# An attention and mixer kernel: a head pair's turned q, k and decay rows reach their operand tiles by plain transfers instead of VectorE copies

## The chip, the cores and the metric

The kernel runs on one core of a Trainium2 chip. The metric is device time in microseconds (us). An execution that is profiled gives, besides its time, a trace of every instruction on the core's engines: TensorE (PE, with its weight loads as PEld), VectorE (DVE), ScalarE (ACT), GpSimd (POOL) and SyncE (SP), and of the transfers that SP and POOL issue. SP computes nothing here; it issues transfers, one after the other, and holds at one that must wait.

## The reference, cut to what matters

Eight batches, eight heads, 576 tokens, 64 elements a head; then a mixer over tokens of low rank (32) and a feed-forward part of width 2048 on the 512 channels.

```python
scores = scale * q @ k.T                       # per batch and head, 576 x 576
cum    = cumsum(max(s, 0))
bias   = -(cum[:, None] - cum[None, :])
scores = where(causal, -1e9, scores + min(bias, 0))
attn   = exp(scores - max) / sum
x      = attn @ v                              # 8 x 576 x 512
u      = x + (x.T @ U @ V).T                   # mixing over tokens
out    = u + max(u @ w_ch1, 0) @ w_ch2
```

## The kernel before, in words

**Pairs.** The 64 heads of all batches are worked in 32 pairs; pair n belongs to batch n // 4. For each pair there is an operand tile, a *slot*: 64 rows of q and of k with the elements on the partitions (turned), and under them four *decay rows*, with which the product of TensorE gives q times k and the cumulated bias at once. From pair 8 on three slots are used in turn, so pair n takes the slot of pair n - 3 and must wait for that pair's scores.

**How a slot is filled.** The decay rows come from a scratch tensor in HBM by two small transfers on SP (`rows_of`, L302). For batches 0 to 3, TensorE turns q and k, and DVE or ACT copies them from PSUM (`transposes`). From pair 16 on (`ZB * PB`, batches 4 to 7) POOL's transfers load q and k of both heads side by side (`load_pairs`, L121), one transposing transfer on SP turns a whole pair (`turn_pair`, L358) into one of three *landings*, tiles of 128 partitions with one head in the lower and one in the upper half, and `part_pair` (L366) copies each half into the slot's lower 64 partitions by a DVE copy.

**The main loop** goes over n from 8 to 33. In iteration n it issues the transposing transfer of pair n + 3, the slot of pair n + 1, the scores of pair n (`scores`, L429; exp on ACT, the causal mask on DVE, L373), and the values of pair n - 1 (`values`, L493, scaled by DVE into `x_sb`, L503). For batches from 2 on, `values` also issues a transposing transfer on SP that turns the pair's x (`xT<-x_sb`, L510), four to a batch. In the second pair of a batch (n = 13, 17, 21, 25, 29), `seqmix` of the batch before runs: PE computes the low-rank product, and DVE adds it to the turned x (L547, `uT<-...,xT`). It needs all four turned x of that batch, the last of which belongs to the pair whose values were computed just before. Between these steps PE is filled with the feed-forward part of an earlier batch (`chanmix`: L662 the first product, L720 the second, by quarters; DVE sums at L698 and L734; sends of the results `out_dram<-o_sb` on SP, L744; the turned u, `u_sd<-uT`, on SP, L1026).

**Who sets the order.** PE and POOL run in the order in which the program is written (`in_program_order` at the end). DVE, ACT and SP are written in program order for batch 0 only; after that the framework's scheduler orders their instructions by data, priority and its own estimates, and the semaphores are placed for that order. On each engine instructions then go strictly in that order: what stands behind a waiting instruction waits too. A transfer on SP also waits for the one eight transfers before it to have landed, since SP has eight completion semaphores in turn.

**Buffers named below.** The results leave through three `o_sb` tiles in turn; a batch group has four quarters, so the fourth quarter's first DVE write waits until the first quarter's send has landed.

Of the kernel before, what the change touches and what calls it, by code (L numbers as in the profile page):

```python
# [16 lines left out]
ALU = mybir.AluOpType  # L17


def in_program_order(tc, first, engines):  # L20

    traced, last = tc.nc.cur_bb.bb.instructions, {}
    for ins in list(traced)[first:]:
        if ins.engine not in engines:
            continue
        prev = last.get(ins.engine)
        if prev is not None:
            tc.add_manual_dep(
                ins,
                prev.name,  # L30
                mybir.DependencyInfo(
                    mybir.DependencyClass.NoSync, mybir.DependencyReason.DATA
                ),
                reason="in_program_order",
            )
        last[ins.engine] = ins


# [1 line left out]
def kernel(  # L40
# [12 lines left out]
    nc = tc.nc  # L53
# [10 lines left out]
    NP = BH // 2  # L64
# [288 lines left out]
    def landing(n):  # L353
        return landings[(n - ZB * PB) % 3]

    def turn_pair(n):
        b, hp = divmod(n, PB)
        nc.sync.dma_start_transpose(  # L358
            out=landing(n).rearrange("p (a m) -> p a m", m=TR),
            in_=by_pairs(b)[:, hp].rearrange("p c t two d -> p (c t two d)"),  # L360
        )

    def part_pair(n):
        rows_of(n)
        for hh in range(2):
            nc.vector.tensor_copy(slot_of(n)[0:D, hh, 0 : 2 * S], landing(n)[ds(hh * D, D)])  # L366
            yield

    def mask(dst, n_tiles, w, on_pool=False):
        if on_pool:  # L370
# [110 lines left out]
    def values(n, pT):  # L481
        b, hp = divmod(n, PB)
        if hp == 0:
            x_of[b] = work.tile([128, PB, 5, 128], BF16, tag="x_sb", name="x_sb")
            if b >= FT:
                xT_of[b] = work.tile([128, 4, 640], BF16, tag="xT", name="xT", bufs=1)
        x_sb, vt = x_of[b], v_slot(b)
        for hh in range(2):
            h = 2 * hp + hh
            po = pwork()[:, : 5 * (D + 1)].rearrange("p (i d) -> p i d", i=5)  # L490
            for i in range(5):
                for j in range(i + 1):
                    nc.tensor.matmul(  # L493
                        po[:, i, :],
                        lhsT=pT[:, hh, ds(place(j, i), 128)],
                        rhs=vt[:, j, h, :],
                        start=(j == 0),
                        stop=(j == i),
                        skip_group_check=True,
                    )  # L500
            rec = work.tile([128, 5, 1], FP32, tag="rec", name="rec", bufs=4)
            nc.vector.reciprocal(rec, po[:, :, D : D + 1])  # L502
            nc.vector.tensor_tensor(  # L503
                x_sb[:, hp, :, ds(hh * D, D)],
                po[:, :, 0:D],
                rec.to_broadcast([128, 5, D]),
                op=ALU.mult,
            )
            if hh == 1 and b >= FT:
                nc.sync.dma_start_transpose(  # L510
                    out=xT_of[b][:, hp, :].rearrange("p (t m) -> p t m", t=5),
                    in_=x_sb[:, hp, :, :].rearrange("p t d -> p (t d)"),
                )
            yield


# [725 lines left out]
    for n in range(2 * PB, NP + 2):  # L1242
# [11 lines left out]
                step(mixing)  # L1254
                fill_with(2)
        if n > 2 * PB and n + 1 < NP:
            for at, _ in enumerate((transposes if n + 1 < ZB * PB else part_pair)(n + 1)):
                step_fill()
                if at == 0:
                    step(mixing)  # L1260
        if 2 * PB + 1 < n < NP:
            for at, _ in enumerate(scores(n, pT_of(n))):
                step_fill()
                if at == 1:
                    step(mixing)
        for _ in mixing:
            fill_with(1)
        if hp == 1 and FT < b < B:
# [76 lines left out]
```

## Time and profile before

| | us |
|---|---|
| median of the runs (lowest, highest) | 357.67 (357.37 to 358.89) |
| the profiled execution's own time | 359.33 |
| its span, first to last instruction | 357.6 |
| PE busy in it | 343.6 |
| DVE busy | 264.4 |
| ACT busy | 207.6 |
| POOL busy | 112.6 |

"Busy" leaves out instructions that only issue transfers or wait; what SP does is therefore read from its own queue's rows. A row of groups such as `L366 DVE COPY slot<-turned 64x1152 ... x12 | 5.7, 478 | 1.0 <-PE pwork L429 0.8` reads: line 366, on DVE, writing `slot` from `turned`, twelve of them, 5.7 us busy in all, 478 ns each, and 1.0 us of idle time of DVE just before them, of which 0.8 ended with PE's line 429. A row of waits such as `A <- B: 3.1, 2, 2.8` reads: A waited for B 3.1 us in all, in two places, 2.8 us at the longest. A row of the chain or of the queue begins with the start and the length in us. The names `qk_sd` in rows of L358 and L366 are two of the three landings, which lie in spare columns of the tiles that hold q and k; `turned` is the third.

### The profile page before, as it was taken

What the parts mean: (1) busy time and instruction counts of PE and PEld (TensorE: products, weight loads), DVE (VectorE), ACT (ScalarE), POOL (GpSimd) and SP (SyncE); (2) the same over time, 40 slices, a digit from 0 to 9 for tenths busy, and PEclk for the clock granted to TensorE, in tenths of its full rate; (3) what the DMA queues carried; (4) which work ended last, traced back from release to release, by engine and by line L of the source; (5) the groups of instructions that cost most, each with busy time, mean ns of one, the idle gap of its engine ahead of it and who ended that gap; (6) DMA issues with size and microseconds to landing.
All of it is one profiled execution on the core that took longest, in us unless ns stands there. A gap on an engine that the chain in (4) does not pass through costs nothing.

```text
span 357.6 us, 9219 instructions
## 1 busy us (share of the span) xinstructions
PE 343.6 (96%) x3770; PEld 247.9 (69%) x3770; DVE 264.4 (74%) x584; ACT 207.6 (58%) x314; POOL 112.6 (31%) x158
## 2 busy tenths in 40 slices
PE   7999999999998999999999997899899999999996
PEld 3685656665587657775678565776588558888885
DVE  8686776779789849883798465983788779676774
ACT  4786965847762577348833874347752554675710
POOL 8897274447356603850366040000000000000000
PEclk9999999999999999999999999999999999999999
DMA  6999999999999999999599999472033525010022
GB/s 100 163 193 203 177 187 121 146 144 97 192 101 171 162 168 88 167 176 159 72 120 160 204 118 90 73 163 57 0 57 83 115 30 120 29 60 31 29 90 88
DMA packets 163713, 42.06 MB, mean 118 GB/s; under 512 B 148312, under 2 KB 162040, under 8 KB 163672
## 3 DMA queue, kind: packets, MB, share of 16 engines
q0 software_dynamic: 101744, 18.45, 80.7%
q1 hardware_dynamic: 61640, 22.83, 36.0%
q8 instruction: 29, 0.48, 0.6%
q10 hardware_dynamic: 288, 0.20, 0.2%
q14 instruction: 12, 0.10, 0.1%
HBM read 37.25 MB, written 9.70 MB: 131 GB/s over the span
## 4 chain that ended last, share of the span: by engine, by line
PE 77%; DVE 12%; ACT 5%; DMA 4%; issue 2%; POOL 0%; DVEq 0%; ACTq 0%; POOLq 0%
PE pwork L662 22%; PE pwork L720 12%; PE quarter L720 9%; PE pscore L429 9%; PE pwork L493 7%; PE parts L950 6%; PE pwork L681 3%; DVE uT L547 3%; DMA xT<-x_sb 2%; ACT pT L447 2%; PE pwork L322 2%; DVE slot L345 2%; DVE o_sb L734 2%; DVE slot L698 2%; ACT hT L1039 1%
## 5 line engine op out<-in xcount | busy, mean ns | idle before, releaser
L662 PE MATMUL pwork<-uT,w_sb 128*128 128x512 bf16 x432 | 106.6, 379 | 1.1 <-ACT hT L1039 0.9
L447 ACT ACTIVATE pT<-pscore 128x1024 bf16<-128x1024 f32 x56 | 56.5, 1031 | 52.7 <-PE pscore L429 52.3
L1039 ACT ACTIVATE hT<-pwork 128x512 bf16<-128x512 f32 x108 | 65.4, 610 | 37.1 <-PE pwork L662 36.3
L662 PEld LDWEIGHTS <-w_sb 128*128 128x128 bf16 x448 | 38.7, 98 | 38.0 <-issue 1.3
L429 PE MATMUL pscore<-slot 68*128 68x320 bf16 (+1 forms) x500 | 55.4, 246 | 0.6 <-ACT hT L447 0.3
L185 POOL DMA_DIRECT2D v_slot<-in_v_dram x40 | 33.8, 860 | 67.9 <-PE pwork L493 57.6
L429 PEld LDWEIGHTS <-slot 68*128 68x128 bf16 x564 | 41.8, 97 | 18.2 <-issue 1.2
L373 DVE TENSOR_TENSOR pT<-pT,keep 128x512 bf16<-128x512 bf16 (+1 forms) x81 | 28.5, 353 | 31.7 <-ACT pT L447 28.7
L720 PEld LDWEIGHTS <-hT 128*128 128x128 bf16 x496 | 46.7, 98 | 7.5 <-issue 0.8
L493 PEld LDWEIGHTS <-pT 128*128 128x128 bf16 x870 | 32.5, 97 | 10.2 <-issue 4.4
L493 PE MATMUL pwork<-v_slot,pT 128*128 128x65 bf16 x870 | 35.8, 193 | 3.8 <-DVE uT L547 3.1
L503 DVE TENSOR_TENSOR x_sb<-pwork,rec 128x320 bf16<-128x320 f32 x64 | 31.2, 489 | 1.5
L459 ACT ACTIVATE pT<-pscore 128x1024 bf16<-128x1024 f32 x29 | 30.4, 1047 | 2.6 <-PE pscore L429 2.4
L720 PE MATMUL pwork<-w_sb,hT 128*128 128x256 bf16 x240 | 30.1, 273 | 0.3 <-DVE o_sb L734 0.3
L345 DVE COPY slot<-pwork 64x576 bf16<-64x576 bf16 x30 | 24.1, 803 | 7.2 <-PE pwork L322 6.8
L121 POOL DMA_DIRECT2D qk_sd<-in_q_dram x32 | 23.8, 743 | 14.0 <-PE pwork L322 4.9
L720 PEld LDWEIGHTS <-slot 128*128 128x128 bf16 x256 | 24.1, 98 | 5.0 <-issue 1.9
L121 POOL DMA_DIRECT2D qk_sd<-in_k_dram x32 | 23.7, 740 | 5.7 <-DMA v_slot<-in_v_dram 1.8
L720 PE MATMUL pwork<-w_sum,slot 128*128 128x256 bf16 x160 | 20.1, 273 | 1.1 <-DVE o_sb L734 1.1
L720 PE MATMUL quarter<-w_sb,hT 128*128 128x256 bf16 x144 | 18.0, 273 | 0.3 <-DVE uT L547 0.3
L681 PE MATMUL pwork<-w_sb,hT 128*128 128x512 bf16 x64 | 16.3, 379 | 0.0
L502 DVE RECIPROCAL rec<-pwork 128x5 f32<-128x5 f32 x64 | 12.0, 189 | 5.4 <-PE pwork L493 5.0
(166 smaller groups left out, 513.7 us busy)
## 6 DMA issues: line engine op xcount, KB each, us to landing
out_dram<-o_sb SPq DMA_DIRECT2D x34, 256.0 KB
v_slot<-in_v_dram POOLq DMA_DIRECT2D x32, 128.0 KB, 7.7
w_sb<-in_moe_w_ch_dram POOLq DMA_DIRECT2D x4, 1024.0 KB, 13.3
qk_sd<-in_q_dram POOLq DMA_DIRECT2D x32, 72.0 KB, 6.0
qk_sd<-in_k_dram POOLq DMA_DIRECT2D x32, 72.0 KB, 5.9
qk_sd<-in_q_dram POOLq DMA_DIRECT2D x4, 288.0 KB, 12.4
qk_sd<-in_k_dram POOLq DMA_DIRECT2D x4, 288.0 KB, 11.5
qk_sd<-in_q_dram POOLq DMA_DIRECT2D x4, 144.0 KB, 5.2
```

Source lines behind the costliest of these rows:

```text
L121: nc.gpsimd.dma_start(out=by_pairs(b)[:, h // 2, c, :, h % 2, :], in_=src[b, h].rearrange("(t p) d -> p t d", p=TR),)
L185: nc.gpsimd.dma_start(out=vt[:rows_t, t, :, 0:D], in_=v[b, :, ds(t * 128, rows_t), :].rearrange("h p d -> p h d"),)
L345: copies(n, hh, par)(in_turn[:, :, :, :, par], src.rearrange("p c t m -> p c m t"))
L373: nc.vector.tensor_tensor(dst, dst, keep[:, :, 0:w].to_broadcast([128, n_tiles, w]), op=ALU.min)
L429: nc.tensor.matmul(dst, lhsT=slot[0:KA, hh, ds(S + j * 128, 128)], rhs=slot[0:KA, hh, lo:hi], start=True, stop=True,)
L447: nc.scalar.activation(pT[:, hh, 0:1024], near, EXP, scale=scale)
L459: nc.scalar.activation(pT[:, :, 1024:1536], mid.rearrange("p (a b) -> p a b", a=2), EXP, scale=scale)
L493: nc.tensor.matmul(po[:, i, :], lhsT=pT[:, hh, ds(place(j, i), 128)], rhs=vt[:, j, h, :], start=(j == 0), stop=(j == i), skip_group_check= ...
L503: nc.vector.tensor_tensor(x_sb[:, hp, :, ds(hh * D, D)], po[:, :, 0:D], rec.to_broadcast([128, 5, D]), op=ALU.mult,)
L662: nc.tensor.matmul(f1, lhsT=w1_sb[:, kt, ds(nf * 128, 128)], rhs=u[:, kt, :], start=(kt == 0), stop=(kt == 3),)
L720: nc.tensor.matmul(acc[:, i, :], lhsT=a[:, kt, ds(i * 128, 128)], rhs=b[:, kt, :], start=(begin and i == 0 and kt == 0), stop=(kt == HF - ...
L1039: nc.scalar.activation(hT[:, nf, :], f1, RELU)
```

## The change

`part_pair` no longer copies on DVE. It issues, after the two transfers of the decay rows, two plain transfers on SP, each of 64 partitions by 1152 elements of two bytes, from the landing's halves to the slot, and chains these four in their order on SP. It is called in iteration n for pair n + 2, after that iteration's scores; before, the scheduler's copy of pair n + 1 stood ahead of them. The two steps of filling that went with the copies stay where they were (`range(2)`). And the transposing transfer of a pair is tied on SP behind the last transposing transfer of x that was written before it (`x_turned`).

```diff
+def after(tc, ins, prev):
+    tc.add_manual_dep(
+        ins,
+        prev.name,
+        mybir.DependencyInfo(mybir.DependencyClass.NoSync, mybir.DependencyReason.DATA),
+        reason="in_program_order",
+    )
...
+    x_turned = []
+
+    def last_sp():
+        return [ins for ins in list(nc.cur_bb.bb.instructions) if ins.engine == E.SP][-1]
+
     def turn_pair(n):
         b, hp = divmod(n, PB)
         nc.sync.dma_start_transpose(
             out=landing(n).rearrange("p (a m) -> p a m", m=TR),
             in_=by_pairs(b)[:, hp].rearrange("p c t two d -> p (c t two d)"),
         )
+        if x_turned:
+            after(tc, last_sp(), x_turned[-1])
 
     def part_pair(n):
+        begin = len(nc.cur_bb.bb.instructions)
         rows_of(n)
         for hh in range(2):
-            nc.vector.tensor_copy(slot_of(n)[0:D, hh, 0 : 2 * S], landing(n)[ds(hh * D, D)])
-            yield
+            nc.sync.dma_start(out=slot_of(n)[0:D, hh, 0 : 2 * S], in_=landing(n)[ds(hh * D, D)])
+        in_program_order(tc, begin, [E.SP])
...
                     in_=x_sb[:, hp, :, :].rearrange("p t d -> p (t d)"),
                 )
+                x_turned.append(last_sp())
...
-            for at, _ in enumerate((transposes if n + 1 < ZB * PB else part_pair)(n + 1)):
+            for at, _ in enumerate(transposes(n + 1) if n + 1 < ZB * PB else range(2)):
                 step_fill()
...
+        if ZB * PB <= n + 2 < NP:
+            part_pair(n + 2)
         for _ in mixing:
             fill_with(1)
```

In the scheduled order of SP, the transposing transfer of a pair now stands behind an x transfer of its iteration, then follow the pair's decay rows and its two plain transfers, which wait for it to have landed, and then the next x transfer. The instructions of PE, ACT and POOL keep their order; DVE's list is shorter by 23 rows (32 copies, some of them side by side), and a few neighbours change places.

More of the change, by code (lines that the diff above doesn't have):

```diff
@@ L27, in in_program_order @@
         if prev is not None:
[L28 to L35, printed above, removed]
+            after(tc, ins, prev)
         last[ins.engine] = ins
```

## The prediction

> **What bounds the kernel now.** I read, in this order, the page's busy shares, the table by stage, the waits, the groups of VectorE (DVE), and then the queue of SyncE (SP) in order of time.
>
> The first part of the page:
>
> ```profile
> PE 343.6 (96%) x3770; PEld 247.9 (69%) x3770; DVE 264.4 (74%) x584; ACT 207.6 (58%) x314; POOL 112.6 (31%) x158
> ```
>
> TensorE (PE) bounds the kernel, so a change pays only where PE is idle. The table by stage, around the four seqmix calls of pairs 13, 17, 21 and 25, in whose stretches the removed copies lie (columns: stretch, its length, then busy time of PE, PEld, DVE, ACT, POOL, clock, DMA share, GB/s):
>
> ```profile
> 104.00:118.00 14.00, 13.10 (x174) 10.95 (x173) 12.38 (x30) 4.00 (x6) 8.68 (x12) 1.00 1.82 161
> 142.00:154.00 12.00, 11.61 (x138) 9.82 (x135) 11.06 (x27) 3.29 (x5) 10.61 (x15) 1.00 2.49 155
> 176.00:190.00 14.00, 13.35 (x165) 11.09 (x163) 13.66 (x33) 4.84 (x7) 10.68 (x15) 1.00 1.71 116
> 210.00:230.00 20.00, 16.39 (x191) 12.52 (x190) 15.11 (x36) 7.22 (x12) 4.21 (x5) 1.00 1.23 78
> ```
>
> PE is idle for 0.90, 0.39, 0.65 and 3.61 us there, 5.55 us in all: the most that these four stages can give back. Between them PE is busy throughout. What ends PE's waits between 100 and 260 us, from the waits of PE and, in the second fence, those of all engines:
>
> ```profile
> PE pwork L493 <- DVE uT L547: 3.1, 2, 2.8
> PE pwork L720 <- DVE o_sb L734: 1.4, 3, 0.8
> PE pwork L592 <- DVE uT L547: 0.6, 2, 0.3
> ```
>
> ```profile
> DVE uT L547 <- DMA xT<-x_sb: 3.3, 1, 3.3
> ```
>
> PE waits for DVE's uT sums (L547), and once, at pair 25, that sum itself waits 3.3 us for the transposing transfer of x (L510). The chain of waits shows that transfer's whole flight:
>
> ```profile
> 214.58 8.62 DMA xT<-x_sb
> ```
>
> The copies that go (DVE groups between 109 and 246 us):
>
> ```profile
> L366 DVE COPY slot<-qk_sd 64x1152 bf16<-64x1152 bf16 x20 | 9.5, 475 | 3.4 <-PE pwork L429 3.1
> L366 DVE COPY slot<-turned 64x1152 bf16<-64x1152 bf16 x12 | 5.7, 478 | 1.0 <-PE pwork L429 0.8
> ```
>
> And the queue into which their successors go, SP in order of time (issue start, issue length):
>
> ```profile
> 139.07 1.31 SPq L358 DMA_TRANSPOSE turned<-qk_sd  x1
> 141.74 1.20 SPq L510 DMA_TRANSPOSE xT<-x_sb  x1
> ...
> 176.98 1.23 SPq L510 DMA_TRANSPOSE xT<-x_sb  x1
> 178.42 2.30 SPq L358 DMA_TRANSPOSE qk_sd<-qk_sd  x1
> ...
> 185.80 0.54 SPq L744 DMA_DIRECT2D out_dram<-o_sb  x1
> ...
> 211.86 2.62 SPq L358 DMA_TRANSPOSE qk_sd<-qk_sd  x1
> 214.58 1.23 SPq L510 DMA_TRANSPOSE xT<-x_sb  x1
> ```
>
> The views print issues, not landings; the completion events of the same trace give those. Pair transfers: 139.07 lands at 144.02, 178.42 at 188.14, 211.86 at 221.30, but 207.33 (no loads beside it) at 210.73. x's: 141.74 lands at 148.13, 176.98 at 184.15, 214.58 at 223.20. So a transfer on SP's queue flies about 3.4 us when POOL's loads are quiet and 6 to 10 us beside them, and POOL's loads start (139.86, 175.35, 210.97) just when the last x of a batch must go.
>
> **The change, part by part.**
>
> *1. The 32 DVE copies go:* 9.5 + 5.7 = 15.2 us of DVE. Most lie where DVE has room and are worth nothing, since PE is busy there. On DVE's full stretches they stand right ahead of L547: 0.71 + 0.56 us (109.3, 110.2) at pair 13; 0.45 + 0.46 (146.1, 146.8) at pair 17; 0.41 + 0.49 and 0.45 + 0.46 (176.1 to 182.4) at pair 21; at pair 25 they come after the wait (226.8, 228.7). Capped by PE's idle time caused by DVE, the gain is 0.8 us at pair 13 (0.28 + 0.30 + 0.24 in PE's rows), at most 0.39 at pair 17, at most 0.65 at pair 21, nothing at pair 25.
>
> *2. 32 plain transfers on SP, 147 KB each.* Not in the trace. The nearest rows are the 256 KB sends of o_sb: issue 0.4 to 0.6 us, flight 2.2 us (226.81 to 229.05, quiet) to 8.1 us (185.80 to 193.90). I take 0.45 us of issue, and 2.3 us of flight in quiet stretches, since they are smaller than the sends; both ends stay for the range. The data itself has cover: the slot is free after scores of three pairs before (the copy of pair 16 ran at 109.3, its first use is near 133.9), some 15 to 24 us, so a few us of flight cost nothing; if SP slid by over 5 us more, the cover of pairs 21 and 25 would go (a rival).
>
> *3. The wait that comes with them.* A DVE copy found its pair long landed. In the new order of SP's queue the two transfers of a pair mostly stand directly behind the pair's own transposing transfer, with only the two row transfers (0.9 us) between, and SP must hold until that one has landed: 3.4 us after its issue when quiet, up to 10 beside loads. Behind the holding SP stand x's next transfer, the sends and u's transfer. A pair now costs SP 3.4 + 2 x 0.45 + 1.3 (x's issue) = 5.6 us quiet, of about 7.5 us between pairs; quiet pairs are covered, the last pair of a batch is not.
>
> *4. The last x of each batch, worked through.* I follow SP from the u transfer on, with the issue lengths and flights above.
> - Pair 17: transfer of pair 19 issued near 137.6, lands 141.6; its two plain transfers to 142.5; x at 142.5 instead of 141.74. The loads have begun, its 640 packets queue behind 128 of the copies, and the trace moves only 634 of SP's packets from 144 to 146 and then almost none until 149. Landing 149.5 to 151 instead of 148.13, wanted at 148.8 (149.73 less the 0.9 us of copies). Pair 25 shows the rate of exchange: DVE's wait of 3.27 us made 2.83 + 0.78 us of PE idle, 0.3 more than the wait, since DVE is behind afterwards. Late by 0.7 to 2.2 is then 1.0 to 2.5 of PE; I take 2.0, less the 0.39 idle already there: +1.6.
> - Pair 21: transfer of pair 23 at 174.3, lands 178.2 to 179; plain transfers to 180; x at 180 instead of 176.98, landing 186.5 to 187.5 instead of 184.15, wanted near 183.8. Late by 2.7 to 3.7; I take the early end, 2.7 + 0.3, less the 0.65 already idle: +2.3. Then pair 24's plain transfers hold SP until about 189, and the send of 185.80 goes at about 189.5; DVE's first write of the fourth quarter (194.25) needs that buffer, and before it landed at 193.90, with 0.35 us to spare. With flights of 5 to 8 us it lands 0 to 3 us late, by which time the uT wait has shifted the need too: some 0.5 more, +2.8.
> - Pair 25: here moving the pair's transfer behind x's helps. Before, 1152 packets stood ahead of x's 640; after, 128 larger ones do. x is issued near 214 to 215.5 and lands at 221 to 222 instead of 223.20: -1 to -2.2; I take -1.0, because the loads' burst of 217 to 220 lets SP's packets hardly through and SP arrives late from pair 21.
> - Pair 29: no loads then; x at 247.85 as before: 0.
>
> *5. What else moves.* SP stood 14.6 us (71 to 86 us) before pair 16's transposing transfer, waiting for k's load; now that transfer goes near 106, and rows, u and x of batch 2 are no longer held. PE is idle 0.16 us from 95 to 100, so that gain is between 0 and 0.2; I take 0. TensorE, ScalarE and POOL keep their instruction order; POOL's loads of q and k wait for later transposing transfers, but their first use is over 15 us later: 0. The 4.7 MB of copies add some 34 GB/s to a DMA stretch of 104 to 182 GB/s; bounded by 0 and 1 us through the loads, taken as 0.
>
> **Sum:** -0.8 + 1.6 + 2.8 - 1.0 = +2.6 us. The profiled execution took 359.33 us (span 357.6 and 1.7 around it), 1.66 above the median of the runs, 357.67; so 361.9 by its time, **360.3 against the median**.
>
> **The rivals.**
> - *F, the queue keeps up:* the copies fly fast, x at pairs 17 and 21 lands no later than before, and at pair 25 in time. Then -0.8 - 0.39 - 0.65 - 2.83 = -4.7: 353.0; with pair 25 half gained, 354.5. For it: quiet pairs have 2 us to spare on SP. Against it: SP's hold falls on exactly the transfers that run into the loads. It decides if pair 23's transposing transfer lands before 177, when the loads' packets begin.
> - *E, the loads leave SP's queue a share, and gain and loss cancel:* in the quiet microsecond from 172 us the trace has 700 of SP's packets; at half of that x's 640 pass in about 2 us at any time. Then pair 17 costs nothing (x lands near 147) and pair 25 gains 2, while pair 21's late issue stays: -0.8 + 0 + 2.8 - 2.0 = 0: 357.7. For it: from 151 to 153 SP moved 1152 packets beside 993 of POOL's. Against it: from 147 us 1130 packets of POOL's queue started in a microsecond and none of SP's, and from 218 us 1174 against 14. [...]
> - *L, the slots come late:* SP slides so far that scores wait for their operands. Copies of pairs 21 and 25 land, by my walk, 4 to 5 us ahead of use; two flights of 10 us instead of 6 use that up and cost 2 to 3 us at each: +2.6 + 5 = 365.3. Against it: flights of 9 to 10 us appear only beside loads, and these pairs' transfers mostly fly before them.
>
> **How the numbers follow.** Forecast S 0.45, F 0.25, E 0.20, L 0.10. S alone spans 358.6 (pair 17 at its low end, pair 25 gaining 1.7) to 361.8 (both x's at their late ends). The range over all cases, 353.8 to 364, leaves out the far end of F and of L, about one in ten each. Half a per cent, 1.8 us, is about what a measurement of this kernel can tell from no change: faster (under 355.9) is nearly all of F and a little of E, 0.26; slower (over 359.5) most of S and all of L, 0.47; within, the rest, 0.27.
>
> **What would show it.** Right: SP's waits list the copies' line waiting for the pair's transfer, some 30 times and 2 to 6 us each; x's last transfer of pair 21's stretch is issued near 180; DVE's L547 waits for xT at pairs 17, 21 and 25; PE's idle rises in 142 to 154 and 176 to 190, falls in 104 to 118. Wrong: L547 never waits for xT, and PE's idle in 210 to 230 falls below 1 us (F); or PE's scores (L429) wait for the copies' transfers (L).

## The result, and the profile after

| | before | after |
|---|---|---|
| median of the runs, us (lowest to highest) | 357.74 (356.70 to 358.89) | 366.95 (364.63 to 372.01) |
| the profiled execution's own time, us | 359.33 | 368.38 |
| its span, us | 357.6 | 366.7 |

The change is slower: the ratio is 1.0247, with an interval of 1.0204 to 1.0290. Medians and ranges here and below are over all executions, while ratios leave out executions that lay more than 1.5% above the fastest of their kernel, so a ratio need not be the quotient of two medians. The profiled executions differ by about as much as the medians (9.1 us of span, 9.2 of medians), so the two traces can be set against each other. First the busy shares on the page of the kernel after:

```profile
PE 345.6 (94%) x3735; PEld 251.0 (68%) x3770; DVE 251.4 (69%) x552; ACT 207.5 (57%) x314; POOL 112.4 (31%) x158
```

VectorE is 13.0 us less busy, as was meant. TensorE has the same matmuls in its program (35 of their records are missing from this trace) and is still 2.0 us longer busy; the mean granted clock is 0.986 in this execution and 1.00 in before's. The table by stage of the kernel after (stretch, length, then busy time of PE, PEld, DVE, ACT, POOL, granted clock, DMA share, GB/s) shows where:

```profile
104.00:118.00 14.00, 13.72 (x191) 11.88 (x189) 12.18 (x30) 3.95 (x6) 8.62 (x12) 1.00 1.83 137
142.00:154.00 12.00, 7.24 (x73) 6.00 (x71) 5.03 (x13) 2.74 (x4) 9.85 (x15) 0.98 2.40 158
154.00:161.00 7.00, 6.32 (x57) 5.11 (x57) 4.75 (x11) 0.00 (x0) 2.71 (x4) 0.55 2.00 206
176.00:190.00 14.00, 13.95 (x154) 9.89 (x153) 10.45 (x24) 10.42 (x16) 7.59 (x10) 1.00 1.12 134
210.00:230.00 20.00, 17.04 (x170) 11.37 (x170) 9.35 (x22) 11.96 (x19) 4.21 (x5) 1.00 1.30 142
230.00:237.00 7.00, 4.35 (x50) 3.72 (x50) 5.13 (x12) 0.00 (x0) 0.00 (x0) 0.76 0.62 137
```

Pair 13 (first row) is idle for 0.28 us instead of 0.90. The loss lies in two places, pair 17 (second and third row) and pair 25 (the last two), and in each the clock falls towards the end of the idle time and stays low behind it. Pair 17 makes everything after it late, so the row from 176 to 190 us is not yet pair 21's stage: that stage lies from 174.55 to 186.33 us before and from 181.13 to 192.04 us after (starts of the same matmuls, the products with v), and PE is idle in it for 0.65 us before and not at all after. The waits of the kernel after between 100 and 260 us name what ended these:

```profile
DVE uT L558 <- DMA xT<-x_sb: 11.7, 2, 5.9
PE pwork L503 <- DVE uT L558: 11.1, 3, 5.5
```

PE waits for DVE's uT sum, and that sum waits for the turned x, twice for almost 6 us. PE's and then DVE's own rows of the kernel after (start, length, and in brackets the idle time ahead of the row) give the two stalls to the hundredth:

```profile
154.69 0.98 PE L503 MATMUL pwork<-v_slot,pT 128*128 128x65 bf16 x15 [5.44 <-DVE uT L558]
...
232.65 0.98 PE L503 MATMUL pwork<-v_slot,pT 128*128 128x65 bf16 x15 [5.49 <-DVE uT L558]
```

```profile
153.88 1.09 DVE L558 TENSOR_TENSOR uT<-pwork,xT 128x320 bf16<-128x320 f32 x3 [5.72 <-DMA xT<-x_sb]
```

Why x is late is seen in SP's queue of the kernel after, in order of time (issue start, issue length):

```profile
138.93 2.35 SPq L365 DMA_TRANSPOSE turned<-qk_sd  x1
141.38 1.11 SPq L304 DMA_DIRECT2D slot<-rows_hbm  x2
146.19 1.13 SPq L376 DMA_DIRECT2D slot<-turned  x2
147.41 1.28 SPq L520 DMA_TRANSPOSE xT<-x_sb  x1
...
219.05 1.98 SPq L365 DMA_TRANSPOSE qk_sd<-qk_sd  x1
221.09 1.34 SPq L376 DMA_DIRECT2D slot<-qk_sd  x1
222.53 1.09 SPq L304 DMA_DIRECT2D slot<-rows_hbm  x2
227.83 1.13 SPq L376 DMA_DIRECT2D slot<-qk_sd  x2
229.06 1.28 SPq L520 DMA_TRANSPOSE xT<-x_sb  x1
```

SP's list ends at 142.49 and goes on at 146.19: it holds for pair 19's transposing transfer, which by the completion events landed at 146.17. x of pair 15, scaled by DVE at 140.67, stands behind it and is issued at 147.41, 6.74 us late. At pair 25 SP holds from 223.62 to 227.83 for pair 27's transposing transfer; x of pair 23, scaled at 218.71, is issued at 229.06, 10.35 us late. The chain of waits of the kernel after has the flights:

```profile
147.41 6.44 DMA xT<-x_sb
...
219.05 8.71 DMA qk_sd<-qk_sd
229.06 2.69 DMA xT<-x_sb
```

And SP's own waits after 100 us say the same in sums:

```profile
SPq L376 <- DMA qk_sd<-qk_sd: 12.6, 4, 5.9
...
SPq L376 <- DMA turned<-qk_sd: 8.6, 3, 4.4
```

The clock behind the stalls, in single microseconds of the kernel after (columns as in the table by stage):

```profile
152.00:153.00 1.00, 0.00 (x0) 0.00 (x0) 0.00 (x0) 0.00 (x0) 1.00 (x2) 1.00 1.36 112
153.00:154.00 1.00, 0.00 (x0) 0.00 (x0) 0.12 (x1) 0.00 (x0) 1.00 (x3) 0.72 1.35 201
154.00:155.00 1.00, 0.32 (x7) 0.31 (x7) 1.00 (x4) 0.00 (x0) 1.00 (x2) 0.50 2.14 184
...
160.00:161.00 1.00, 1.00 (x11) 0.85 (x10) 0.00 (x0) 0.00 (x0) 0.00 (x0) 0.87 1.84 196
161.00:162.00 1.00, 1.00 (x14) 0.83 (x12) 0.94 (x2) 0.50 (x1) 0.00 (x0) 1.00 2.17 306
```

PE has its work back at 154.69 and runs at half clock until about 160.3, for 5.6 us. Behind the second stall the same lasts from 232.65 to about 235.4, for 2.7 us.

PE's order is the same in both kernels, so the sum can be taken between the starts of the same products with v in the two traces. The stage of pair 13 is 0.96 us shorter. The stage of pair 17 is 4.99 us longer (16.67 instead of 11.68), and the two stretches behind it, at half clock, 1.15 and 1.48 us. The stage of pair 21 is 0.88 us shorter. The stage of pair 25 is 2.66 us longer (16.59 instead of 13.93), and the next stretch, at half clock, 1.16; the one after that is 0.83 us shorter, since before's wait of 0.78 us for `o_sb` is gone. Together this is 8.77 of the 9.1 us of span; all other stretches make the 0.3 us left. Of it the low clock is 3.8 us: 1.15 + 1.48 + 1.16.

### The profile page after: what moved, and what is told of

It reads as the page before. It is cut to its first block, busy times and chain, and to the rows that moved or that the text cites. A ratio compares the mean times of both kernels' runs of the same rounds, so it can differ in the third digit from the quotient of the medians.

```text
span 366.7 us, 9187 instructions
## 1 busy us (share of the span) xinstructions
PE 345.6 (94%) x3735; PEld 251.0 (68%) x3770; DVE 251.4 (69%) x552; ACT 207.5 (57%) x314; POOL 112.4 (31%) x158
## 4 chain that ended last, share of the span: by engine, by line
PE 80%; DMA 6%; DVE 6%; ACT 4%; issue 3%; SPq 0%; DVEq 0%; ACTq 0%; POOLq 0%
PE pwork L673 22%; PE pwork L731 14%; PE quarter L731 10%; PE pscore L439 9%; PE pwork L503 8%; PE parts L961 6%; PE pwork L692 3%; DMA xT<-x_sb 2%; DMA qk_sd<-qk_sd 2%; PE pwork L324 2%; DVE uT L558 2%; DVE slot L347 2%; ACT pT L457 1%; PE pscore L400 1%; ACT hT L1050 1%
## 5 line engine op out<-in xcount | busy, mean ns | idle before, releaser
L673 PE MATMUL pwork<-uT,w_sb 128*128 128x512 bf16 x405 | 104.6, 379 | 2.5 <-ACT hT L1050 0.9
L503 PE MATMUL pwork<-v_slot,pT 128*128 128x65 bf16 x870 | 37.0, 196 | 11.9 <-DVE uT L558 11.1
L503 PEld LDWEIGHTS <-pT 128*128 128x128 bf16 x870 | 33.8, 99 | 18.6 <-issue 12.6
L731 PE MATMUL pwork<-w_sb,hT 128*128 128x256 bf16 x240 | 31.2, 279 | 0.0
L731 PE MATMUL pwork<-w_sum,slot 128*128 128x256 bf16 x160 | 21.0, 280 | 0.0
L558 DVE TENSOR_TENSOR uT<-pwork,xT 128x256 bf16<-128x256 f32 (+6 forms) x30 | 11.0, 415 | 11.7 <-DMA xT<-x_sb 11.7
```

What stands on the lines that cost most here:

```text
L503: nc.tensor.matmul(po[:, i, :], lhsT=pT[:, hh, ds(place(j, i), 128)], rhs=vt[:, j, h, :], start=(j == 0), stop=(j == i), skip_group_check= ...
L673: nc.tensor.matmul(f1, lhsT=w1_sb[:, kt, ds(nf * 128, 128)], rhs=u[:, kt, :], start=(kt == 0), stop=(kt == 3),)
L731: nc.tensor.matmul(acc[:, i, :], lhsT=a[:, kt, ds(i * 128, 128)], rhs=b[:, kt, :], start=(begin and i == 0 and kt == 0), stop=(kt == HF - ...
```

## The experiments

Ratios are to the kernel before, run beside it on the same chip, with their 95% intervals. "Scaled", "issued" and "landed" are the end of DVE's scaling of x, the start of the transfer's issue on SP, and its last completion event.

### The order without the plain transfers, and the plain transfers without the order

```diff
 # order_only: the change, with the copies back on DVE
-            nc.sync.dma_start(out=slot_of(n)[0:D, hh, 0 : 2 * S], in_=landing(n)[ds(hh * D, D)])
+            nc.vector.tensor_copy(slot_of(n)[0:D, hh, 0 : 2 * S], landing(n)[ds(hh * D, D)])
+            yield
```

> The kernel before, with one half of the change: a pair's transposing transfer goes behind x's, and the copies into the slot stay on VectorE. Theory H (SP's hold: the plain transfers wait on SP for their pair's transposing transfer, and x's transfer stands behind them): nothing holds SP here, so x's last transfer of a batch goes as soon as x is scaled; PE's idle at pair 25 (3.6 us before) falls below 1 us, no drop of the granted clock, 353 to 356 us. Rival O (the new place of the transposing transfers does the harm, since they now fly beside POOL's loads): slower than before, 360 us or more, with x's transfer landing late at pair 17 too.

Measured: 388.53 us, 1.0878 (1.0851 to 1.0906). Theory H's number is off by over 30 us. The waits of this kernel between 100 and 260 us:

```profile
DVE slot L375 <- DMA qk_sd<-qk_sd: 20.6, 7, 7.1
...
PE pwork L602 <- DVE uT L557: 19.3, 3, 7.9
```

Tied behind x, the transposing transfers are issued later, and some fly beside the loads (105.44, 151.89, 196.00 and 243.45 us, with flights of 8.3 to 10.5 us; the others take 3.2 to 4.8). DVE's copy of the pair is next in DVE's list and holds DVE for up to 7.1 us, and uT and the scaling of x stand behind it. So the tie and the plain transfers belong together: with the copies on DVE the late transfers hold DVE, with the change they hold SP.

```diff
 # copies_only: the change, without the tie
-        if x_turned:
-            after(tc, last_sp(), x_turned[-1])
```

> The other half alone: plain transfers in place of the VectorE copies, the transposing transfers early as in the kernel before. In SP's order a pair's transposing transfer then stands two or more x transfers ahead of its plain transfers. Theory H: the plain transfers find their pair landed, SP holds for less than 1 us each, x's last transfer at pair 17 goes within 1.5 us of x being scaled, no drop of the clock at pair 17; pair 25 as before or a little worse, 355 to 359 us. Rival T (the 4.7 MB of added traffic is what makes x's transfers late): as slow as the changed kernel, 364 to 368 us.

Measured: 372.23 us, 1.0419 (1.0382 to 1.0456), worse than with the tie. SP's waits in this kernel:

```profile
SPq L365 <- DMA slot<-qk_sd: 23.2, 11, 5.4
...
SPq L365 <- DMA slot<-turned: 14.4, 7, 5.4
```

The wait has moved: a transposing transfer that comes early finds its landing still being read by the plain transfers of three pairs before, and holds SP until they have landed. A DVE copy frees a landing in 0.48 us (the mean in the kernel before); a plain transfer in 2.3 to 9.0 us in this kernel. x of pair 15, scaled at 140.80, is issued at 146.45 here too.

### Everything behind x, and the wait with copies left on DVE

```diff
 # copies_behind_x: the change, a pair's rows and plain transfers tied behind x and written after the mixing
+        traced = nc.cur_bb.bb.instructions
+        after(tc, [ins for ins in list(traced)[begin:] if ins.engine == E.SP][0], x_turned[-1])
...
-        if ZB * PB <= n + 2 < NP:
-            part_pair(n + 2)
         for _ in mixing:
             fill_with(1)
+        if ZB * PB <= n + 2 < NP:
+            part_pair(n + 2)
```

> The changed kernel with all its traffic, but the decay rows and the two plain transfers of pair n + 2 are tied behind the x transfer of the values of pair n - 1, one iteration later, so that their pair's transposing transfer was issued an iteration before them. Theory H: SP's waits for the transposing transfers fall from 21 us to under 6 us, x's last transfer at pair 17 goes within 1 us of x being scaled, PE's idle there below 1 us, no clock drop; VectorE's relief stays; 353 to 357 us. Rival T: 363 us or more.

Measured: 369.44 us, 1.0337 (1.0294 to 1.0380). uT no longer waits for xT anywhere (x of pair 15: scaled 141.45, issued 141.48), but scores wait for slots instead. The waits of this kernel:

```profile
PE pscore L441 <- DMA slot<-qk_sd: 6.2, 5, 3.1
...
PE pscore L441 <- DMA slot<-turned: 2.6, 2, 1.9
```

That is rival L of the prediction, which the change itself does not show: with the plain transfers of all pairs later, their slots are late.

```diff
 # hold_only: the change; the plain transfers carry 16x8 elements into a small tile, and DVE copies the pair
-            nc.sync.dma_start(out=slot_of(n)[0:D, hh, 0 : 2 * S], in_=landing(n)[ds(hh * D, D)])
+            nc.sync.dma_start(out=held[:, ds(hh * 8, 8)], in_=landing(n)[0:16, ds(hh * 8, 8)])
+        for hh in range(2):
+            nc.vector.tensor_copy(slot_of(n)[0:D, hh, 0 : 2 * S], landing(n)[ds(hh * D, D)])
```

> The changed kernel with its SP order, but each plain transfer cut to 16 partitions by 8 elements into a spare tile, and the slot filled by the VectorE copies as before: the hold without the traffic, and without VectorE's relief. Theory H: x's last transfers of pairs 17 and 25 are held as long as in the changed kernel (6 to 10 us after x is scaled), PE idles some 5 us at both and the granted clock drops after them; 365 to 369 us. Rival T: the waits go with the traffic, 356 to 359 us.

Measured: 391.30 us, 1.0976 (1.0923 to 1.1030). DVE waits for the transposing transfers as without the plain transfers (23.7 us in 8 places and 9.3 in 3), so this run mixes two waits and says nothing of SP's alone.

### Keeping TensorE busy in the stalls

```diff
 # spin_in_stalls
         if 2 * PB < n <= NP:
+            if n in (17, 25):
+                dst = pscore()
+                for _ in range(8):
+                    spin(1, dst[:, 0:512])
+                    spin(1, dst[:, 512:1024])
             run(values(n - 1, pT_of(n - 1)))
```

> The changed kernel with 16 matmuls of 128x512 that wait for no transfer, put in TensorE's order right ahead of the values of pairs 16 and 24, where it stands still for 5.44 and 5.49 us; their sums go into a spare score buffer and are not used. Theory C (a stall longer than 4 to 5 us halves the granted clock, and that is paid on top of the stall): idle at each place falls to 1 to 2 us, the clock stays at 1.00 in the stretches 149 to 161 and 227 to 236 us, and the time is 362.5 to 364 against 366.95 for the change alone. Rival N (the low clock is not from the stall, or costs nothing): the stalls are filled with work that nobody needs, the clock dips all the same or nothing is won, 366 to 368.

Measured: 366.20 us, 1.0239 (1.0173 to 1.0305), no different from the change. The table by stage of this kernel:

```profile
142.00:154.00 12.00, 10.71 (x98) 7.67 (x97) 5.78 (x15) 2.43 (x4) 9.62 (x15) 1.00 2.08 149
...
176.00:190.00 14.00, 12.44 (x147) 9.64 (x147) 10.48 (x24) 6.75 (x11) 10.38 (x14) 1.00 1.78 143
190.00:210.00 20.00, 18.51 (x207) 13.91 (x209) 12.03 (x30) 9.42 (x14) 5.42 (x8) 0.91 1.56 199
...
230.00:237.00 7.00, 7.00 (x87) 5.86 (x86) 5.97 (x12) 1.97 (x3) 0.00 (x0) 1.00 0.50 120
```

At pairs 17 and 25 the stall falls to 1.23 us and to nothing, and the clock stays at 1.00, as theory C has it. (Its limit of 4 to 5 us, an estimate that lies between before's stall of 2.83 us without a fall and the change's of 5.44 us with one, does not hold: the table at the end has falls behind stalls of 1.23 and 1.50 us.) But the time is not won: a new stall of 2.89 us stands at pair 21, with its own fall of the clock. x of pair 19 is scaled 3.7 us earlier than in the change (179.62 against 183.33), but SP holds and issues it at 183.09, and it lands at 190.56; in the change it landed at 189.96, and nobody waited. So the low clock went with the stalls here (1.00 in 142 to 154 and 230 to 237 us), but beside a late x its price was not won back by itself here: the next batch's x took what was won.

### x of a batch's last pair first

```diff
 # batch_x_first: the change, and
+        if n % PB == PB - 1:
+            traced = nc.cur_bb.bb.instructions
+            after(tc, [ins for ins in list(traced)[begin:] if ins.engine == E.SP][0], x_turned[-1])
         in_program_order(tc, begin, [E.SP])
```

> The changed kernel, but the plain transfers of the last pair of each batch (19, 23, 27, 31) are tied behind the transposing transfer of x four pairs back (15, 19, 23, 27), so that x of a batch's last pair no longer stands behind SP's wait for a pair's transposing transfer. Theory Q (the loss is that wait in front of the last x of a batch): uT's wait for xT at pair 17 is gone (5.7 us before), that at pair 25 is under 3 us, no clock dip near 155, 355 to 359. Rival L (the plain transfers that now go later miss their slots): scores of pairs 19 or 27 wait 2 to 6 us for slots, with a clock dip behind, 361 to 367.

Measured: 361.02 us, 1.0113 (1.0078 to 1.0148). Of the 2.47% that the change costs, this gives back about half, by moving four pairs' rows and plain transfers behind an x. The waits at pairs 17 and 25 are gone (x of pair 15 scaled 140.13, issued 140.16; of pair 23 216.44 and 216.47), and 142 to 154 us is full. The stage table of this kernel shows where the rest is:

```profile
176.00:190.00 14.00, 9.80 (x97) 8.11 (x96) 8.54 (x20) 3.33 (x5) 8.79 (x13) 0.85 1.81 142
```

Again pair 21, a stall of 4.20 us: x of pair 19 is issued at 177.55, right behind the transposing transfer of pair 23 (175.06), and flies 9.25 us. Theory Q was right on pairs 17 and 25 and missed this, so its time, 359 at most, is 2 us short; rival L's wait of scores does not appear.

```diff
 # x_first_all: batch_x_first, and the last pair's transposing transfer behind the same x
+        if n % PB == 3:
+            late.append(last_sp())
...
                 x_turned.append(last_sp())
+                if hp == PB - 1 and late:
+                    after(tc, late.pop(), x_turned[-1])
```

> The changed kernel with both the transposing transfer and the plain transfers of the last pair of each batch behind x of four pairs back; the run with only the plain ones there took 361.02 us and stalled 4.2 us at pair 21, with x of pair 19 issued right behind the transposing transfer of pair 23 and 9.25 us in flight. Theory Q (what stands ahead of that x on SP's queue is the loss): x of pair 19 flies 6.5 to 7.5 us, the stall at pair 21 falls under 2 us and the clock stays at 1.00, 355.5 to 358.5. Rival L (now the slots of pairs 19, 23, 27 come late): scores wait 2 us or more for slots, 360 to 365.

Measured: 362.99 us, 1.0180 (1.0109 to 1.0251), not better. x of pair 19 has pair 23's transposing transfer behind it now, is issued at 177.72 and still flies 9.68 us. Theory Q is refuted at this point: the transposing transfer directly ahead of x is not what makes it fly long there. Rival L's reason isn't seen either (no wait of scores for a slot). Close ahead of it went two plain transfers of another pair (175.06 to 176.19) and x of pair 18 (176.29); in the kernel before, where that x flew 7.17 us, only rows of another pair stood there (173.43).

### The traffic alone, and the issue alone

```diff
 # traffic_only: the kernel before, and behind x of pairs 12 to 27
+                for at in range(2 if 12 <= 4 * b + hp < 28 else 0):
+                    nc.sync.dma_start(
+                        out=spare[4 * b + hp, ds(at * D, D)], in_=w1_sb[ds(at * D, D), 0, 0 : 2 * S]
+                    )
 # issue_only: the same with
+                        out=spare[4 * b + hp, ds(at * D, 16), 0:16], in_=w1_sb[ds(at * D, 16), 0, 0:16]
```

> The kernel before, with its VectorE copies and the old place of the pairs' transposing transfers, and 32 more plain transfers of the size of the change's (64x1152, two behind each x of pairs 12 to 27), out of a weight tile, whose data is there from the start, into memory outside the core that nobody reads. They wait for no transfer. Theory Q (not the bytes and the issue on SP but SP's wait costs the time): 356.6 to 359. Rival T (the bytes beside the loads and the issue slow the rest): 361 or more, with longer flights of x and uT waiting for xT.

> The kernel before, with 32 tiny plain transfers (16x16) on SP's queue in the very places of the 32 large ones of the run with the traffic alone, which took 365.47 us (its profiled execution 361.51). Theory I (the issue on SP, some 0.6 us each, pushes x of a batch's last pair back: 143.47 instead of 141.74 at pair 17): most of that loss stays, 360 to 364. Rival Y (the bytes lengthen the flight of x beside the loads, 8.21 instead of 6.39 us): the loss is gone, 356.5 to 358.5, with x of pair 15 landing by 149.

Measured: 365.47 us, 1.0240 (1.0176 to 1.0304) with the bytes; 357.69 us, 1.0034 (0.9988 to 1.0080) with the issue alone. So rival T was right and theory Q wrong: bytes that nobody waits for cost as much as the whole change, and SP's 32 issues cost little. The two traces have the same list on SP and can be read line against line. With the bytes SP falls back from transfer to transfer even ahead of the loads: u's issue at 122.6 takes 5.79 us instead of 4.80, and the next three pairs' transposing transfers go at 129.75, 135.74 and 141.28 instead of 128.52, 134.06 and 139.22. The last one meets the loads, and x of pair 15 behind it is issued at 143.47 and lands at 151.67, after 8.21 us, instead of 141.38, 147.94 and 6.57 us. PE stalls for 2.22 us at pair 17, and the clock falls. This trace is of the fastest of the five executions, 361.51 us; what the slower ones lose beyond that (up to 366.96 us) is not seen.

### The wait and the bytes, in the change's own order

These three keep SP's list as it is in the change, but for three plain transfers that the two runs without the bytes issue ahead of an x and a transposing transfer instead of behind them. They leave out the filling of the operands of pairs 16 to 31, or fill them with weights.

```diff
 # wait_no_bytes
-            nc.sync.dma_start(out=slot_of(n)[0:D, hh, 0 : 2 * S], in_=landing(n)[ds(hh * D, D)])
+            nc.sync.dma_start(out=slot_of(n)[0:16, hh, 0:16], in_=landing(n)[ds(hh * D, 16), 0:16])
 # bytes_no_wait
+            nc.sync.dma_start(out=slot_of(n)[0:D, hh, 0 : 2 * S], in_=w1_sb[ds(hh * D, D), 0, 0 : 2 * S])
 # neither
+            nc.sync.dma_start(out=slot_of(n)[0:16, hh, 0:16], in_=w1_sb[ds(hh * D, 16), 0, 0:16])
```

> The changed kernel, every instruction of SP in its place, but each plain transfer carries 16x16 elements instead of 64x1152, out of the same landing, so that SP waits as before and the bytes are gone. The operands of pairs 16 to 31 are not filled (their q, k and decay columns stay those of older pairs), so that part of the computation is left out. Theory H (SP's wait for the pair's transposing transfer in front of x): x of pair 15 is issued 4 us or more after its scaling, uT waits for xT 2 us or more at pair 17, 358 to 363. Rival Y (the bytes make the flights long, and without them the wait is short): no wait of uT for xT over 1 us, 353.5 to 356.5.

> The changed kernel, every instruction of SP in its place, but the plain transfers take 64x1152 elements out of a weight tile that is there from the start, so that the bytes stay and SP doesn't wait. Pairs 16 to 31 get weights for operands; the computation on the turned q and k is left out. Theory H: x of pair 15 goes within 2 us of its scaling, no stall over 1 us at pair 17, 354 to 357.5. Rival Y (the bytes): flights of x of 8 us or more beside the loads, stalls of 2 us or more at pairs 17, 21 or 25, 359 to 366.

> The changed kernel, every instruction of SP in its place, with plain transfers of 16x16 elements out of a weight tile: no wait and no bytes, and no copies on VectorE (operands of pairs 16 to 31 left as they were, as in the run with the wait alone). Both theories: no stall of uT at pairs 17, 21 and 25 over 1 us, TensorE's idle in 104 to 118 at 0.3 us, 353 to 355.5. If it is above 357, the place of the transposing transfers behind x costs by itself, by neither wait nor bytes.

| | no bytes | bytes |
|---|---|---|
| no wait | 356.75 us, 1.0001 (0.9967 to 1.0035) | 363.23 us, 1.0176 (1.0133 to 1.0219) |
| wait | 362.27 us, 1.0113 (1.0037 to 1.0189) | the change: 366.95 us, 1.0247 (1.0204 to 1.0290) |

Each alone is a loss, the bytes perhaps the larger one (their intervals overlap), and together they come to nearly the sum, 2.47% against 1.13 + 1.76. Neither theory was right alone. The four executions with the wait alone fall into two groups, 359.15 and 360.05 us, and 364.49 and 364.75; the trace below is of the 360.05.

In this trace the wait alone strikes at pair 21, not at 17. SP's queue of that kernel, and DVE's wait in it between 100 and 300 us:

```profile
172.88 1.27 SPq L365 DMA_TRANSPOSE qk_sd<-qk_sd  x1
174.25 1.50 SPq L304 DMA_DIRECT2D slot<-rows_hbm  x2
179.60 1.17 SPq L376 DMA_DIRECT2D slot<-qk_sd  x2
180.86 1.23 SPq L520 DMA_TRANSPOSE xT<-x_sb  x1
```

```profile
DVE uT L558 <- DMA xT<-x_sb: 4.7, 1, 4.7
```

SP holds from 175.75 to 179.60 for pair 23's transposing transfer (landed 179.58); x, scaled at 174.55, goes at 180.86 and lands at 187.06. At pair 17 the transposing transfer of pair 19 went at 136.25, ahead of the loads, and landed in 3.35 us. In the change it went at 138.93 and needed 7.23: the bytes had pushed SP back by 2.7 us, and that was enough to carry the wait into the loads. So at pair 17 the bytes make the wait longer, though over the whole kernel the two losses do not come to more than their sum.

The bytes alone strike at pairs 17 and 25: x of pair 15 issued at 142.04 with a flight of 8.29 us (stall 2.23 us), x of pair 23, scaled at 214.08, issued at 222.51 (stalls of 1.50 and 2.01 us).

With neither there is still one stall, of 3.38 us at pair 21. SP's queue of that kernel:

```profile
174.41 1.48 SPq L365 DMA_TRANSPOSE qk_sd<-qk_sd  x1
175.99 1.55 SPq L304 DMA_DIRECT2D slot<-rows_hbm  x2
177.60 1.95 SPq L377 DMA_DIRECT2D slot<-w_sb  x2
179.65 1.23 SPq L523 DMA_TRANSPOSE xT<-x_sb  x1
```

SP holds for no transfer here; the five issues of one pair, 5 us, stand in front of an x that was scaled at 175.43 and goes 4.2 us later. So a third part, the mere place of the issues, can cost 3.4 us at pair 21, and what the change wins at pairs 13 and 25 (no stall there) can pay for it. The profiled execution, 359.23 us, is at the upper end of that kernel's runs (354.70 to 359.24); its median, 356.75, lies between the 355.5 and the 357 of the expectation, and equals that of the kernel before.

### What was meant to help: one transfer moved, and VectorE relieved elsewhere

```diff
 # one_turn_behind_x: the kernel before, and in turn_pair
+        if n == 30:
+            after(tc, last_sp(), x_turned[23])
```

> The kernel before, with its VectorE copies, and only the transposing transfer of pair 30 moved behind that of x of pair 23 (it stood just ahead of it, issued at 211.86). Theory P (part of the 8.62 us that x of pair 23 flies is the 1152 packets of that transfer ahead of it and 2.6 us of SP's issue): x issued near 212 to 213, landed 217 to 220 instead of 223.20, TensorE's idle in 210 to 230 falls from 3.61 to 0.5 to 2 us, 353.5 to 355.5 against 356.6 to 357.7. Rival B (POOL's loads hold x whatever stands ahead of it): landing after 221.5, no difference within 0.5 %, 356 to 358.

Measured: 355.60 us (355.22 to 356.31), 0.9947 (0.9916 to 0.9978), half a per cent faster than the kernel before, with 1 outside the interval. x of pair 23 is issued at 212.15 and lands at 217.99 after 5.84 us, as theory P had it, though the time is 0.1 above its range; PE's stage of this kernel, with 3.61 us idle before:

```profile
210.00:230.00 20.00, 19.54 (x238) 15.65 (x236) 18.44 (x44) 9.08 (x14) 4.21 (x5) 1.00 0.91 101
```

A caution: in the run with the issue alone pair 30's transfer still stood ahead of that x (210.28, x at 212.48), and it landed at 219.18 without a stall. So the 2.83 us at pair 25 in the profiled execution of before are not in every execution; that execution, 359.33, lay above its median.

```diff
 # plain_16: one_turn_behind_x, and in part_pair
+            if n == 16:
+                nc.sync.dma_start(out=slot_of(n)[0:D, hh, 0 : 2 * S], in_=landing(n)[ds(hh * D, D)])
+            else:
 # act_copies: one_turn_behind_x, and in part_pair
+            copy = nc.scalar.copy if n in (16, 20, 23, 24) else nc.vector.tensor_copy
+            copy(slot_of(n)[0:D, hh, 0 : 2 * S], landing(n)[ds(hh * D, D)])
```

> The kernel with the one moved transposing transfer (355.60 us) and, besides, only the two copies of pair 16 by plain transfers; they ran on VectorE at 108.74 and 109.61, in the stretch of pair 13. Their data has landed 15 us before, so nothing holds SP. Theory G (the prediction's first step: a copy is worth its time only where VectorE holds TensorE back): TensorE's idle in 104 to 118 falls from 0.79 to 0.2 to 0.4 us, the time is 354.8 to 355.4. Rival Z (SP's two issues cost it elsewhere): 355.6 to 356.5.

> The kernel with the one moved transposing transfer (355.60 us), and the copies of pairs 16, 20, 23 and 24, which stand in VectorE's full stretches, made by ScalarE, which is busy for 3.4 of 14, 3.1 of 12 and 4.4 of 14 us there. Theory G (relief of VectorE pays there, and a copy on an idle engine needs no queue of transfers): TensorE's idle in 104 to 118, 142 to 154 and 176 to 190, 1.83 us in all, falls by 0.8 to 1.5, 354.0 to 354.9. Rival A (ScalarE holds its copies in order ahead of the exponentials that scores wait for): 355.6 to 358.

Measured: 357.36 us (354.30 to 359.29), 1.0008 (0.9960 to 1.0056) with pair 16's plain transfers; 354.09 us (353.88 to 354.59), 0.9934 (0.9907 to 0.9961) with the copies on ScalarE. The first wins its 0.5 us at pair 13 (13.72 us busy of 14, as in the change) and gives it back: the next transposing transfer into the same landing waits until the plain ones have landed (115.90) and goes at 116.11 instead of 110.09, SP is behind from there on, and x of pair 15 lands at 150.23 instead of 147.47, with a stall of 1.58 us. Theory G was right on the stage and wrong on the whole.

On ScalarE a copy takes 1.15 us, from the groups of that kernel, instead of 0.48 on VectorE in the kernel before, and the stages of pairs 13, 17 and 21 are idle for 0.31, 0.28 and 0.21 us, 0.80 together instead of 1.83:

```profile
L383 ACT COPY slot<-qk_sd 64x1152 bf16<-64x1152 bf16 x6 | 6.9, 1151 | 0.1
```

```profile
104.00:118.00 14.00, 13.69 (x179) 11.52 (x177) 12.03 (x29) 5.58 (x8) 8.41 (x12) 1.00 1.82 161
142.00:154.00 12.00, 11.72 (x139) 10.09 (x137) 10.27 (x25) 5.46 (x7) 10.69 (x16) 1.00 2.33 169
176.00:190.00 14.00, 13.79 (x159) 11.77 (x157) 12.57 (x28) 7.57 (x10) 10.74 (x16) 1.00 1.97 149
```

This is the fastest kernel of the study, within what theory G expected. Against the one with the moved transfer alone the medians differ by 1.5 us, but they ran on different chips and the intervals of their ratios overlap, so that step is not settled.

## Why the prediction was wrong

It forecast 360.3 us with a range to 364.0; the change takes 366.95. The direction and the kind of loss were right; sizes, places and one term were not. Of its sum of +2.6 us, the stages came out so: pair 13 -0.96 for -0.8, pair 17 +7.6 with the clock for +1.6, pair 21 -0.9 for +2.8, pair 25 +3.0 with the clock for -1.0. Two of the four have the wrong sign, and the loss at pair 25 was not foreseen. That the total came out on the side that was forecast is owed to pair 17 and in part to luck. By its steps:

- **Step 1, the copies that go.** Right: 0.62 us of idle time gone at pair 13, of 0.8 forecast. At pair 21 the 0.65 us are gone too, the most that it allowed there; it had not counted on them, because it expected a late x.
- **Step 2, the plain transfers.** Issue mostly 0.5 to 0.6 us instead of 0.45, flight 2.3 to 2.6 us in quiet stretches and up to 7.4 beside loads: the flight is inside the bounds. The conclusion that their flight costs nothing was the error. It asked only whether the slot is filled in time. That the landing is occupied longer (the run without the tie, and the one with pair 16 alone) and that the bytes slow SP's other transfers was not asked.
- **Step 3, the wait.** Right in kind, and the right transfers. The list of waits shows 7 long ones of up to 5.9 us, 21.2 us together, where it spoke of some 30 of 2 to 6 us.
- **Step 4, pair 17: +1.6.** This is the main failure. It let pair 19's transposing transfer go near 137.6 and land at 141.6, a quiet flight. It went at 138.93, and POOL's loads, issued from 139.86 in the kernel before, were issued from 138.82, ahead of it; it landed at 146.17. The flight of about 4 us became 7.2, x went at 147.41 instead of 142.5, and PE's idle time in that stage is 5.05 us more, not 1.6 more. The text itself had both flights, 3.4 us quiet and 6 to 10 beside loads, and put this transfer on the quiet side without pricing the other.
- **Step 4, pair 21: +2.8.** Not in the change's trace, yet the mechanism appears elsewhere: the delay from pair 17 is so large that x of pair 19 is scaled only at 183.33 and then meets a free SP. With the wait and no bytes, where pair 17 does not stall, x goes at 180.86 and lands at 187.06: the prediction said 180 and 186.5 to 187.5. The stall is 4.47 us there, not 3.
- **Step 4, pair 25: -1.0.** Wrong sign: the stage is 2.66 us longer, and the clock adds 1.16. It took x of pair 23 to be ahead of the transposing transfer that went before it. Pair 30's was moved behind it; but pair 27's, tied only to x of pair 22, stands there with its two plain transfers, and flies 8.71 us (219.05).
- **Step 4, pair 29: 0.** Nothing seen against it.
- **Step 5, the traffic: 0 out of 0 to 1 us.** Put at nothing, and the largest error next to pair 17. In the change's own order the bytes alone cost 1.76%, 6.3 us on 356.7, and on the kernel before 2.40%. A mean rate of 34 GB/s more says nothing of what a late transfer meets.
- **The clock: no term.** 3.8 us behind the two stalls. The granted clock was 0.50 from 153.44 to 160.27 us and from 231.95 to 235.36 us; PE had work in 5.6 and 2.7 us of that. The prediction's own stalls, 2 to 3 us, made the term look needless; before's stall of 2.83 us had left the clock at 1.00.
- **The rivals.** F, a queue that keeps up, is refuted by the two stalls. E, by whose estimate half of the quiet microsecond's 700 packets of SP get through beside the loads, is refuted as an average: at pair 17, from 144 to 149 us, 1188, 1095, 1105, 786 and 980 packets of POOL's queue started in successive microseconds, and 34, 7, 4, 0 and 0 of SP's, although the last of pair 19's transfer was under way until 146.17 and the two plain transfers were issued by 147.32. L is not in the change; it appears when the plain transfers are all put later.

So of the 9 us, the runs show the causes to be two, the wait on SP and the bytes beside the loads, each a loss alone, and at pair 17 the bytes make the wait longer. How the bytes slow SP's issues ahead of the loads was seen (1.2, 1.7 and 2.1 us from pair to pair) and not taken further apart. Why x of pair 19 flies 9.25 and 9.68 us in two of the runs is open.

## What to carry to other kernels

A copy moved from a compute engine to a transfer queue is not free because its destination is needed late: follow the queue to the next transfer that somebody waits for, and price three things ahead of it, the wait for the copy's source, the issues, and the bytes, each at the flight that holds once the big loads have begun. A slip of 2.7 us into such loads doubled a flight here (3.35 to 7.23 us), and the stall of 5.44 us behind it cost 2.6 us more in clock. Before moving work to a queue, look for a compute engine that is idle in that very stretch: eight copies on ScalarE took the idle time of three stages from 1.83 to 0.80 us.

## What the runs showed of the hardware that was not expected

The fall of the clock came in steps in these runs. Taking the granted clock in half microseconds, 1 less the clock, summed over time from the stall on, comes to nothing, 1.71 us, 3.42, or once 5.12; at a clock of one half that is 3.4, 6.8 or 10.2 us of low clock (3.41 and 6.83 us in the change's trace). Among the shorter stalls, how long PE stood still hardly decided it (a selection; the other stalls behind 100 us come with the same steps):

| PE still, us | kernel | 1 less the clock, summed, us |
|---|---|---|
| 7.86 | the order without the plain transfers | 5.12 |
| 5.49 | the change, pair 25 | 1.71 |
| 5.44 | the change, pair 17 | 3.42 |
| 4.47 | wait, no bytes | 3.42 |
| 4.20 | x of the batch first | 3.42 |
| 3.38 | neither | 1.71 |
| 2.89 | matmuls in the stalls, pair 21 | 1.71 |
| 2.83 | before, pair 25 | 0 |
| 2.23 | bytes, no wait, pair 17 | 1.71 |
| 2.22 | the traffic alone, pair 17 | 1.71 |
| 2.01 | bytes, no wait, pair 25 | 0 |
| 1.97 (and 1.21 shortly before) | x first, the last pair's transposing transfer behind it, pair 21 | 3.42 |
| 1.94 | everything behind x | 1.71 |
| 1.58 | pair 16 by plain transfers | 0 |
| 1.50 | bytes, no wait, pair 25 (first gap) | 1.71 |
| 1.23 | everything behind x, a later stall | 1.71 |
| 1.23 | matmuls in the stalls, pair 17 | 0 |

So no single length of a stall divides those with a fall from those without: gaps of 1.23 and 1.50 us went with a fall, and one of 2.83 us did not. By these sums a stall of 1 to 3 us was worth its length here, and sometimes up to 1.71 or 3.42 us more. Why a gap so short went with a fall was not tested.

The second is the spread. The two kernels with the one moved transfer and no plain ones repeated within 1.1 us (355.22 to 356.31, and 353.88 to 354.59), while the kernel before ranged over 4.7 and 5.2 us beside them (355.31 to 360.02, and 355.18 to 360.39), and the one with pair 16's plain transfers over 5.0. Why was not taken apart. One profile of the kernel before therefore shows one of several outcomes.
